# Loading the first segment's query and key weights in two pieces each from one queue

## The chip, the cores and the metric

The kernel runs on one core of a Trainium2 chip. The metric is the device time of one execution in microseconds. Six executions of the kernel before were timed; their median is 254.56 us, the lowest 253.71 and the highest 255.07.

## What is computed

A transformer block with conditioned normalization, on one sequence of 2048 rows of width 448, all in bfloat16:

```python
mod = silu(c) @ w_mod                       # six vectors of 448: sa, ca, ga, sb, cb, gb
h = layernorm(x) * (1 + ca) + sa
x = x + ga * A(h, wq, wk, wv, wo, beta)     # attention
h = layernorm(x) * (1 + cb) + sb
x = x + gb * B(h, w_gate, w_up, w_down)     # (sigmoid(h @ w_gate) * (h @ w_up)) @ w_down
```

The attention A has 16 heads of width 28 and works on 4 segments of 512 rows. Within a segment it is causal softmax attention; besides, each segment reads a memory (a 28 by 28 matrix and a vector for each head) that the segments before have written, and the two results are mixed by sigmoid(beta). The weights wq, wk, wv and wo are 448 by 448 each. w_gate and w_up are 448 by 1792, w_down is 1792 by 448.

## The kernel before

The engines' instruction streams are laid out by hand. Each engine works its stream off in order; semaphores that the framework inserts hold an instruction until its operands are there. A transfer (DMA) is issued by SP or by ScalarE from its own stream, so an issue stands behind whatever is ahead of it there. The framework signals the completion of transfers on eight semaphores that take turns: a transfer is issued only when the one that had its semaphore before, eight transfers earlier in the order that the framework settled, has landed.

A width of 448 is handled as four chunks of the contraction: three of 128 rows and one of 64 (`LW`). The work is staged by segment. For each segment x is normalized and transposed to hT, then q, k and v are projected (`proj_qk`, line 338, `proj_v`, line 350), then for each group of four heads the logits, their exponential, the mask and the product with v follow; the second half of the block follows a segment later, filled in between the attention steps from a list of jobs whose costs and due times are constants in the code (`tick`, `later`, `run_fill`). None of these constants depends on a transfer.

The change lies in the start, in the first 17 us. Lines 106 to 124 issue the first loads: the conditioning vector c_col on ScalarE, two tiles of x on SP and two on ScalarE, and the modulation weights wm for ca and sa in halves, one half on each queue. ScalarE then computes a tanh of c_col (line 126). Lines 151 to 156 load wq, wk and wv: wq and wk into staging tiles `wq_st` and `wk_st`, which lie in the memory that w_down is loaded into later (so the profile names them `wd_sb`), wv into its place. In the kernel before, wq and wk come in three pieces each, chunks 0 and 1, chunk 2, and chunk 3. All of wk's are issued by SP, of wq's the first by SP and the other two by ScalarE.

While these come in, PE runs 20 matmuls without use for their result (`warm_up`, line 645), VectorE normalizes the first four tiles of x (lines 672 to 684), PE computes the modulation columns (`mod_cols`, line 215) and transposes the normalized tiles (`ln0_tr`, line 687). Then the weights are prepared:

```python
    for k in range(2):
        pad_copy(nc.vector, wq_sb, wq_st, k)
    ln0_tr(2)
    ln0_tr(3)
    for kc in range(NK):
        ln0.pe_evac(pts[kc], kc, True)
        if kc == 1:
            pad_copy(nc.vector, wq_sb, wq_st, 2)
    evac_q, evac_k = bias_rows((wq_st, wk_st))
    pad_copy(nc.vector, wq_sb, wq_st, 3)
    warm_up(1)
```

`pad_copy` (line 650, profiled at line 657) scales one chunk of a weight by the modulation and spreads it into heads of 32 columns. `bias_rows` (line 659, profiled at line 664) multiplies the shift vector sa with all four chunks of wq and wk on PE, chunk by chunk, so it reads wq chunk k and wk chunk k side by side. The two rows that result are copied into the 65th row of chunk 3 of `wq_sb` (`evac_q`, on ScalarE) and of `wk_sb` (`evac_k`, on VectorE; both profiled at line 668). wk's four `pad_copy` stand between the two. The first projections (lines 712 and 713) follow, then the same for wv (lines 714 to 719), then the loads of x for segments 1 and 2 (lines 720 and 721). All later loads are issued by SP: beta and wm for ga (line 732), wo (line 160), the last segment of x, w_down (line 746), and w_gate and w_up (lines 741 and 742).

Of the kernel before, what the change touches and what calls it, by code (L numbers as in the profile page):

```python
# [13 lines left out]
P = 128  # L14
# [3 lines left out]
def kernel(  # L18
# [16 lines left out]
    nc = tc.nc  # L35
    _, S, D = A_x.shape
# [7 lines left out]
    DP, LW = NK * P, D - 3 * P  # L44
# [92 lines left out]
    wq_st = wd_sb[:, 0:NK, :]  # L137
    wk_st = wd_sb[:, NK:2 * NK, :]

    def load_w(eng, dst, w):  # L140
        eng.dma_start(dst[:, 0:3, :], w[0:3 * P, :].rearrange("(k p) n -> p k n", p=P))
        eng.dma_start(dst[0:LW, 3, :], w[3 * P:D, :])
# [6 lines left out]
    for b in wm_bufs:  # L149
        nc.vector.memset(b[:, NK * D:], 0.0)  # L150
    for st, w in ((wq_st, A_wq), (wk_st, A_wk)):
        other = nc.scalar if w is A_wq else nc.sync
        nc.sync.dma_start(st[:, 0:2, :], w[0:2 * P, :].rearrange("(k p) n -> p k n", p=P))
        other.dma_start(st[:, 2, :], w[2 * P:3 * P, :])
        other.dma_start(st[0:LW, 3, :], w[3 * P:D, :])
    load_w(nc.sync, wv_sb, A_wv)

    def load_wo():
# [557 lines left out]
    for k in range(NK):  # L716
        r = P if k < 3 else LW
        w = wv_sb[0:r, k, :]
# [156 lines left out]
```

## Time and profile before

| What | Value |
|---|---|
| median of six timed executions | 254.56 us (253.71 to 255.07) |
| the profiled execution, its own time | 254.45 us |
| its span, first to last instruction | 252.7 us |
| mean granted clock of TensorE | 0.993 |
| busy: PE, VectorE, ScalarE, GpSimd | 242.2, 173.8, 139.0, 73.8 us |
| moved by transfers | 19.66 MB, of which 17.61 MB on q1 (SP's queue) and 1.72 MB on q10 (ScalarE's) |
| moved in the first 40 us | 10.26 MB, 257 GB/s on average |

A profile is one execution, and its times run from the start of the span. In a timeline a line holds the start, the duration, the engine, the line of the code, the operation, and output and input; SPq and ACTq are the issues of transfers by SP and ScalarE, PEld are PE's weight loads, and DVE is VectorE. What stands in brackets is the idle time before, and who ended it. A transfer's issue is short; when its data has landed is read from the semaphore events of the trace. The DMA queues are called q1 and q10 there.

### The profile page before, as it was taken

To read this page: it belongs to the slowest core of one execution; us is meant where nothing else is said; L and a number is where in the kernel's file an instruction comes from. 1 tells how busy PE (TensorE), PEld (TensorE's weight loads), DVE (VectorE), ACT (ScalarE), POOL (GpSimd) and SP (SyncE) were. 2 spreads that over 40 slices of the span, in tenths; PEclk is the share of its full clock that TensorE was granted. 3 is DMA by queue.
4 is the path that set the end of the run, shared out by engine and by line. 5 is a ranking of instruction groups with operands and counts; after the bars stand their busy time and mean duration, and the time that the engine had idled before them with its cause. 6 is when DMAs were issued, how large, how long until landed. Compare 5 with 4: busy or idle time off the path is not lost.

```text
span 252.7 us, 5315 instructions
## 1 busy us (share of the span) xinstructions
PE 242.2 (96%) x2059; PEld 115.1 (46%) x2083; DVE 173.8 (69%) x419; ACT 139.0 (55%) x173; POOL 73.8 (29%) x140
## 2 busy tenths in 40 slices
PE   7999999999987999999999999999999999999995
PEld 2534545446533345445434355454344455333454
DVE  6878799874987686389868666895565486544412
ACT  2158879988894978575466857552653300133300
POOL 4359144233552221335613141471120023000000
PEclk9999999999997999999999999999999999999999
DMA  5999996495034212102532210113210015100011
GB/s 151 290 261 250 354 275 112 87 184 72 3 64 66 48 38 21 23 0 44 99 79 44 42 23 0 23 31 92 57 22 3 0 23 119 36 0 0 3 36 36
DMA packets 41168, 19.66 MB, mean 78 GB/s; under 512 B 30008, under 2 KB 40248, under 8 KB 41144
## 3 DMA queue, kind: packets, MB, share of 16 engines
q1 hardware_dynamic: 38408, 17.61, 31.6%
q10 hardware_dynamic: 2736, 1.72, 2.4%
q8 instruction: 16, 0.26, 0.4%
q14 instruction: 8, 0.07, 0.1%
HBM read 10.67 MB, written 1.84 MB: 49 GB/s over the span
## 4 chain that ended last, share of the span: by engine, by line
PE 51%; DVE 7%; POOL 1%; issue 1%; DMA 1%; ACT 1%; DVEq 0%; POOLq 0%
PE ups L559 13%; PE dps L574 13%; PE gps L542 12%; PE gps L547 5%; PE acc L451 3%; PE pwo L510 2%; PE lg L424 2%; DVE fT L562 1%; DVE st L269 1%; DMA hT<-xn 1%; DVE x_sb L520 1%; DVE t L482 1%; PE dM L397 1%; PE ups L547 1%; PE mem L475 1%
## 5 line engine op out<-in xcount | busy, mean ns | idle before, releaser
L427 ACT ACTIVATE pT<-lg 128x2048 bf16<-128x2048 f32 (+1 forms) x48 | 76.8, 1601 | 25.8 <-PE lg L424 25.5
L562 DVE SCALAR_TENSOR_TENSOR fT<-tt,ups 128x512 bf16<-128x512 f32 x56 | 37.3, 687 | 40.4 <-PE ups L559 38.5
L550 ACT ACTIVATE tt<-gps 128x512 f32<-128x512 f32 x56 | 30.4, 594 | 56.4 <-PE gps L547 56.4
L437 POOL TENSOR_SCALAR_AFFINE_SELECT pT<-pT 128x512 bf16<-128x512 bf16 x64 | 40.6, 651 | 70.1 <-ACT pT L427 70.1
L574 PE MATMUL dps<-wd_sb,fT 128*128 128x448 bf16 (+1 forms) x238 | 43.7, 342 | 0.0
L542 PE MATMUL gps<-hT,wg_sb 128*128 128x512 bf16 x155 | 41.0, 387 | 1.6 <-DVE hT L291 0.6
L559 PE MATMUL ups<-hT,wu_sb 128*128 128x512 bf16 x165 | 40.6, 381 | 0.4 <-issue 0.3
L574 PEld LDWEIGHTS <-fT 128*128 128x128 bf16 x238 | 22.9, 98 | 18.7
L542 PEld LDWEIGHTS <-wg_sb 128*128 128x128 bf16 x168 | 15.9, 99 | 18.6 <-issue 1.3
L559 PEld LDWEIGHTS <-wu_sb 128*128 128x128 bf16 x168 | 14.1, 97 | 21.7 <-issue 7.9
L451 PE MATMUL acc<-vt,pT 128*128 128x29 bf16 x640 | 18.6, 175 | 2.0 <-POOL pT L437 1.7
L269 DVE BATCH_NORM_STATS2 st<-x_sb 128x6 f32<-128x448 bf16 x32 | 19.7, 616 | 0.5
L451 PEld LDWEIGHTS <-pT 128*128 128x128 bf16 x640 | 17.7, 96 | 5.1 <-POOL pT L437 2.4
L547 PE MATMUL ups<-hT,wgu_sb 64*128 64x512 bf16 x56 | 18.1, 389 | 0.8 <-ACT tt L550 0.5
L273 POOL TENSOR_SCALAR rs<-mv 128x1 f32<-128x1 f32 (+2 forms) x21 | 5.3, 251 | 44.8 <-DVE mv L270 43.7
L424 PE MATMUL lg<-qT,kT 28*128 28x512 bf16 (+3 forms) x256 | 17.3, 302 | 0.3 <-ACT pT L427 0.2
L547 PE MATMUL gps<-hT,wgu_sb 64*128 64x512 bf16 x56 | 17.2, 388 | 0.1
L343 PE MATMUL pq<-hT,wq_sb 128*128 128x512 bf16 x59 | 16.3, 379 | 0.5 <-issue 0.3
L343 PE MATMUL pq<-hT,wk_sb 128*128 128x512 bf16 x62 | 16.3, 379 | 0.1
L576 DVE TENSOR_TENSOR ot<-dps,x_sb 128x448 bf16<-128x448 f32 (+1 forms) x17 | 9.9, 591 | 9.0 <-PE dps L574 9.0
L277 DVE TENSOR_SCALAR xn<-x_sb,mv,rs 128x448 bf16<-128x448 bf16 x32 | 14.4, 471 | 2.3 <-POOL rs L274 2.3
L274 POOL TENSOR_TENSOR rs<-rs,mhalf 128x1 f32<-128x1 f32 (+2 forms) x21 | 14.2, 674 | 1.8
(101 smaller groups left out, 258.0 us busy)
## 6 DMA issues: line engine op xcount, KB each, us to landing
wm<-in_w_mod_dram SPq DMA_DIRECT2D x4, 392.0 KB, 5.7
x_sb<-in_A_x_dram SPq DMA_DIRECT2D x3, 448.0 KB, 5.7
wd_sb<-in_B_w_down_dram SPq DMA_DIRECT2D x3, 448.0 KB, 9.5
wg_sb<-in_B_w_gate_dram SPq DMA_DIRECT2D x3, 448.0 KB, 9.8
wu_sb<-in_B_w_up_dram SPq DMA_DIRECT2D x3, 448.0 KB, 10.2
out_dram<-ot SPq DMA_DIRECT2D x8, 112.0 KB, 1.8
out_dram<-ot ACTq DMA_DIRECT2D x7, 112.0 KB, 1.7
wm<-in_w_mod_dram SPq DMA_DIRECT2D x2, 196.0 KB
```

What stands on the lines that cost most here:

```text
L269: nc.vector.bn_stats(st[:], self.srcs[i])
L343: nc.tensor.matmul(pq[:, 0:L], lhsT=head_cols(w_sb, k, hc), rhs=h[:, k, :], start=(k == 0), stop=(k == NK - 1))
L424: nc.tensor.matmul(lg[:, hs, wid:wid + nq], lhsT=kT[r, hc, kb * P:(kb + 1) * P], rhs=qT[r, hc, kb * P:L], start=True, stop=True, tile_posi ...
L427: nc.scalar.activation(pT[:, :, w0:w0 + wid], lg[:, :, 0:wid], AF.Exp, scale=scale)
L437: nc.gpsimd.affine_select(out=blk, in_=blk, compare_op=ALU.is_ge, fill=0.0, base=0, pattern=[[0, 4], [1, P]], channel_multiplier=-1)
L451: nc.tensor.matmul(accv[:, qb, hs, 0:ME], lhsT=pT[:, hs, c0:c0 + P], rhs=vt[:, kb, hc * 4 + hs, 0:ME], start=(kb == 0), stop=(kb == qb))
L542: nc.tensor.matmul(g[:, 0:L], lhsT=wg_sb[:, k, f], rhs=h[:, k, :], start=(k == 0), stop=False)
L547: nc.tensor.matmul(dst[:, 0:L], lhsT=wgu_sb[r:r + LW, f], rhs=h[r:r + LW, 3, :], start=first, stop=not first, tile_position=(r, 0))
L550: nc.scalar.activation(tt[:], g[:, 0:L], AF.Tanh, scale=0.5)
L559: nc.tensor.matmul(u[:, 0:L], lhsT=wu_sb[:, k, f], rhs=h[:, k, :], start=False, stop=(k == 2))
L562: nc.vector.scalar_tensor_tensor(ft[:], tt[:], 1.0, u[:, 0:L], op0=ALU.add, op1=ALU.mult)
L574: nc.tensor.matmul(dp[:, c], lhsT=fT_of[(s, fc)][:, t * P:(t + 1) * P], rhs=wd_sb[:, fc, c], start=(fc == 0), stop=(fc == NFC - 1))
```

## The change

wq and wk come in two pieces each instead of three: one of chunks 0 to 2 and one of chunk 3 with its 64 rows. The order is wq's large piece, wk's large piece, wq's small piece, wk's small piece, and SP issues all four. ScalarE issues no transfer any more after the modulation weights until the outputs of the last segments. The destinations and everything that reads them are as before.

```diff
     for st, w in ((wq_st, A_wq), (wk_st, A_wk)):
-        other = nc.scalar if w is A_wq else nc.sync
-        nc.sync.dma_start(st[:, 0:2, :], w[0:2 * P, :].rearrange("(k p) n -> p k n", p=P))
-        other.dma_start(st[:, 2, :], w[2 * P:3 * P, :])
-        other.dma_start(st[0:LW, 3, :], w[3 * P:D, :])
+        nc.sync.dma_start(st[:, 0:3, :], w[0:3 * P, :].rearrange("(k p) n -> p k n", p=P))
+    for st, w in ((wq_st, A_wq), (wk_st, A_wk)):
+        nc.sync.dma_start(st[0:LW, 3, :], w[3 * P:D, :])
     load_w(nc.sync, wv_sb, A_wv)
```

## The prediction

> **What bounds the kernel now.** I read the page first: engine shares and slices.
>
> ```profile
> PE   7999999999987999999999999999999999999995
> PEclk9999999999997999999999999999999999999999
> ...
> DMA  5999996495034212102532210113210015100011
> ```
>
> Each digit is a fortieth of the span. By the page's first part TensorE (PE) is busy for 242.2 us, 96% of the span; after the first slice it has one weak spot, slices 12 and 13 (76 to 88 us), where its granted clock falls too. The DMA engines are full from about 2 us on, in the stage this change touches. An edit to the loads is therefore worth what it does to the start of PE's work, unless it empties or fills a hole later. So I went next to the waits of PE: over the whole run no transfer is named in them; the longest is that weak spot (us in total, times, longest).
>
> ```profile
> PE acc L451 <- POOL pT L437: 1.7, 1, 1.7
> ```
>
> A wait of under 0.2 us doesn't get a line there, so I read the timeline of the first 17 us, the DMA issues first.
>
> ```profile
> 2.38 0.47 SPq L153 DMA_DIRECT2D wd_sb<-in_A_wq_dram  x1
> 4.63 0.38 SPq L153 DMA_DIRECT2D wd_sb<-in_A_wk_dram  x1
> 5.06 0.47 SPq L154 DMA_DIRECT2D wd_sb<-in_A_wk_dram  x1
> 6.08 0.56 SPq L155 DMA_DIRECT2D wd_sb<-in_A_wk_dram  x1
> ...
> 6.36 0.35 ACTq L154 DMA_DIRECT2D wd_sb<-in_A_wq_dram  x1
> 8.12 0.52 ACTq L155 DMA_DIRECT2D wd_sb<-in_A_wq_dram  x1
> ```
>
> wq's last rows are issued last, from ScalarE's queue at 8.12, after all of wk. The trace names the semaphore of each issue: eight take turns, so each transfer waits until the eighth before it has landed. The 8.12 issue waited for half of the first modulation load (landed 8.10, by the semaphore events), the 6.36 issue for another (6.34). In the same way wk's first piece waited for c_col (4.62). wq's last rows land at 12.42. Their readers on VectorE (DVE) and PE:
>
> ```profile
> 11.38 0.42 DVE L306 COPY hT<-lntr 128x512 bf16<-128x512 bf16 x1
> 11.72 0.33 DVE L657 TENSOR_SCALAR wq_sb<-wd_sb,cols 128x448 bf16<-128x448 bf16 x1
> 11.97 0.42 DVE L306 COPY hT<-lntr 128x512 bf16<-128x512 bf16 x1
> 12.45 0.33 DVE L657 TENSOR_SCALAR wq_sb<-wd_sb,cols 64x448 bf16<-64x448 bf16 x1
> ...
> 12.32 0.22 PEld L664 LDWEIGHTS <-sa_bf 64*1 64x1 bf16 x2 [0.38 <-issue]
> ...
> 12.47 0.35 PE L664 MATMUL warm<-wd_sb,sa_bf 64*1 64x448 bf16 x2
> ...
> 15.59 0.08 PEld L664 LDWEIGHTS <-sa_bf 64*1 64x1 bf16 x1 [0.38 <-issue]
> ```
>
> Both start 24 and 42 ns after the landing. Without a wait they would start sooner: the first hT copy is followed after 0.34 us (11.38 to 11.72), the second only after 0.48 (11.97 to 12.45), so DVE stood 0.14 us. On PE, wv's rows have the same step with its data long there (landed 12.84): its last matmul starts 2 ns after its weight load at 15.59, wq's 147 ns after its own at 12.32. So PE stood 0.145 us. That is the only place where I find a consumer waiting for these loads.
>
> [...]the two ScalarE issues cost 0.35 + 0.52 us there. [...]from 6.3 to 6.5 us q1 (SP) moved 49 packets and q10 (ScalarE) 22. [...]The trace shows one such stretch of 3.41 us at half clock, after a stretch with 1.92 us of PE work.
>
> **The change part by part.** Durations are of the profiled execution: 254.45 us, of which 252.7 are span and 1.75 lie around it; it is 0.11 below the median of 254.56.
>
> *ScalarE's two issues go.* 0.87 us leaves its queue at 6.36 to 8.65. Its next work is the hT copy at 11.44, which waits for PE's transposes (6.6 us idle). Worth nothing.
>
> *SP's issues.* Four for wq and wk before (0.47, 0.38, 0.47, 0.56), four after. SP pays nothing more.
>
> *When the pieces land.* I count 896-byte rows in order of issue. Up to the modulation loads 1408 rows are ahead, in both kernels. Before: wq's first piece ends at row 1664 (landed 9.06), wk's at 1920 (9.80), 2048 (10.26), 2112 (10.69), wq's third 128 rows at 2240 (10.88), wv at 2624 (12.11), wq's tail at 2688 (12.42), wv's tail at 2752 (12.84). After: wq's 384 rows end at 1792, wk's at 2176, the tails at 2240 and 2304, wv at 2688 and 2752. Reading these from the same curve (estimates): wq 9.06 + 128 rows at 347 rows per us = 9.43; wk about 10.8; a 64-row tail took 0.3 to 0.44 us behind its forerunner, so wq's tail 11.2 and wk's 11.6 at the late end; wv 12.8 and 13.2. Their issues don't hold them up: wk waits for c_col as before (4.63), the tails for the first two x loads (5.06, 6.08), wv for modulation loads (6.64, 7.46).
>
> *Who needs them.* wq's first rows: DVE at 10.71, 1.3 us later. They land 0.37 later than before, hidden by the normalization and modulation work that DVE does until 10.86. wk: the bias rows on PE at 11.66, 0.9 us after; it lands 1.0 us later than wk's first piece did, and that 0.9 is all the cover. Beyond it each late us costs one. wq's tail: 12.31, margin 1.1. wk's tail: 12.32, margin 0.7. wv: 14.79, margin 1.6.
>
> *The wait that goes.* 0.145 us on PE and 0.14 on DVE, side by side, so counted once. What follows hangs on it step by step: warm matmul 12.75, evacuation of the q row on ScalarE 13.18, last q weights 13.75, k row on DVE 13.79, last k weights 14.47, kT copy 15.04, wv rows 14.93, next projection 15.87. Each is released by the one before, or follows in its queue without a gap; none of them waits for a transfer. So all move up 0.145. What is late next is PE's own step between weight loads of different height (0.28 us) and DVE's copies: no further gain.
>
> *Two transfers fewer, so the turns of the eight semaphores shift.* x for segments 1 and 2 are issued at about 8.10 and 8.80 instead of 9.33 and 9.97, beta at 9.43 instead of 10.52; the next modulation load still waits for PE's transposes (11.15), and from there each transfer has the same forerunner as before. Segment 1's x lands at 14.04 before and by 14.4 after; DVE wants it at 15.50. Does SP stall on a full queue? It issued at once with 2432 rows outstanding (17.40) and took 2.57 us with 2832 (17.83). At 8.80 the new kernel has 3776 issued less 1408 landed, 2368: no. If it did, beta, modulation and wo loads would slip, the first of them wanted at 22.1 us (beta, on ScalarE; landed 15.97). DMA total traffic is the same, and the gate and up weights land at 39 us, wanted from 79. Nothing.
>
> Sum: -0.145 us; 254.45 becomes 254.3, and the median 254.56 becomes 254.4. The bounds of the one unknown cost, DMA timing: in an execution where PE's clock rises earlier than at 7.37 us, the chain could reach wq's tail sooner, at most 0.25 more before DVE and GpSimd's normalization binds (norm at 10.03 to 10.42 against the sa copy at 10.70); where it rises later, the 0.145 vanishes. So -0.4 to 0, and I take the profiled value.
>
> **Rivals.** *A, forecast:* 254.4, own range 254.0 to 254.8.
>
> *B, the wait changes owner:* wk's tail, now behind wq's, lands as late as wq's did (12.4), and the bias row waits for it instead: 254.56. For: tails of 64 rows are slow for their size. Against: it would need 0.8 us more than estimated.
>
> *C, faster through the clock:* PE's half-clock stretch disappears.
>
> ```profile
> 72.22:75.64 3.42, 2.61 (x21) 1.10 (x18) 2.82 (x9) 3.42 (x5) 2.62 (x5) 1.00 0.30 61
> 75.64:79.05 3.41, 1.92 (x44) 1.32 (x44) 2.07 (x6) 2.98 (x4) 2.06 (x4) 1.00 0.42 87
> 79.05:82.46 3.41, 3.18 (x9) 0.87 (x10) 3.15 (x11) 0.08 (x1) 0.00 (x0) 0.50 0.41 38
> ```
>
> The stretches, with PE busy first after their length and the clock third from the end: 1.92 of 3.41 us busy (56%) was followed by half clock, 2.61 (76%) was not. A program 0.145 us earlier puts less of the hole at 74.83 to 76.50 into the window: 60%. If the limit lies between, 3.18 us of PE work runs at full clock: -1.6, giving 252.8. [...]
>
> *D, slower, through one mechanism:* the time to land grows with the size of a piece. wq's first piece took 6.7 us for 224 KB; at 336 KB in proportion 10.0, landing at 12.4 where DVE wants it at 10.71. Both q pads slip by 1.7, less the 0.145: 254.56 + 1.5 = 256.1. It decides from a landing after 10.71. Against: wv's 336 KB piece took 4.6 us (7.48 to 12.11); the 6.7 was queueing.
>
> That the change isn't what it says can hardly be: each piece is an instruction of its own.
>
> **How the numbers follow.** 0.3% of 254.56 is 0.76 us, about what a measurement of this kernel can tell from no change. A 0.46 and B 0.12 lie within it: same 0.58. C 0.25: faster. D 0.17: slower. The range reaches from C's time down to A's and B's: 252.7 to 255.4, leaving out D.
>
> **What would show it.** Right: no ScalarE issue of wq; the pad of wq's tail 0.34 us after the hT copy and the bias matmul right at its weight load; the first logits at 16.7 instead of 16.84. Wrong: DVE's first pad after 10.8, or a bias row at 11.66 that waits for wk (D); a gap before the last bias matmuls (B); full clock at 79 us (C).

## The result and the profile after

The changed kernel takes 253.64 us in the median of 34 timed executions (252.95 to 254.33). The kernel before, run beside it, has a median of 254.18 us (71 executions), and beside the experiments 254.09 to 254.23 in four sets of 19 to 51, all 0.3 to 0.5 below the median of the six that were shown first. The ratio of after to before is 0.9977, 95% interval 0.9967 to 0.9986: 0.58 us less, between 0.36 and 0.84. A later set of the changed kernel gave 0.9978 (0.9963 to 0.9993). The forecast was 254.4, 0.145 us below the time before: its sign is right, its size is a quarter of what came.

The profiled execution of after takes 253.97 us, with a span of 252.3 and a mean granted clock of 0.991. The page's slices of after:

```profile
PE   7899999999988999999999999999999999999995
PEclk9999999999997999999999999999999999999999
...
DMA  5999996493036330102331210113210015100011
```

The picture is the old one: one weak spot in slices 12 and 13, where the clock falls. The longest wait of PE that the kernel itself can do something about is still the mask at that spot, now line 450.

```profile
PE acc L450 <- POOL pT L436: 1.7, 1, 1.7
```

The issues of wq and wk in the timeline of after (start, duration, queue):

```profile
2.38 0.47 SPq L152 DMA_DIRECT2D wd_sb<-in_A_wq_dram  x1
4.65 0.38 SPq L152 DMA_DIRECT2D wd_sb<-in_A_wk_dram  x1
5.08 0.56 SPq L154 DMA_DIRECT2D wd_sb<-in_A_wq_dram  x1
5.98 0.47 SPq L154 DMA_DIRECT2D wd_sb<-in_A_wk_dram  x1
```

By the semaphore events they land at 9.30, 10.70, 10.96 and 11.35, wv at 12.20 and 12.51. The readers of wq's last rows, on VectorE (DVE) and on PE:

```profile
11.74 0.41 DVE L305 COPY hT<-lntr 128x512 bf16<-128x512 bf16 x1
12.07 0.32 DVE L656 TENSOR_SCALAR wq_sb<-wd_sb,cols 64x448 bf16<-64x448 bf16 x1
```

```profile
1.42 6.51 PE L646 MATMUL warm<-qT,ident 128*128 128x512 bf16 x20 [1.42 <-POOL mhalf L168]
...
11.43 1.01 PE L663 MATMUL warm<-wd_sb,sa_bf 128*1 128x448 bf16 x8
...
16.46 0.40 PE L423 MATMUL lg<-qT,kT 28*128 28x512 bf16 x4
```

The pad now follows the copy after 0.33 us, as every other pad does, where it was 0.48: the wait is gone. All eight bias matmuls run as one group without a hole. The first logits stand at 16.46, against 16.84 before, which is 0.38 and not 0.145. The other 0.23 comes from the clock: the 20 matmuls at the start took 6.51 us here and 7.41 in the profile before, because PE's clock rose at 5.55 instead of 7.37, and so the last hT copy starts at 11.74 instead of 11.97. That is not the change's doing; the rise differs from execution to execution, from 4.38 us (seventh experiment) to 7.37 in the profiles. It does show how little one profile says of this wait: the chain that reads wq's tail was ready 0.23 us sooner here.

At the weak spot the stretches of after are these (PE busy first after the length, clock third from the end):

```profile
70.41:73.82 3.41, 3.41 (x24) 1.60 (x22) 2.76 (x9) 3.41 (x5) 1.16 (x3) 1.00 0.27 55
73.82:77.23 3.41, 1.74 (x51) 1.25 (x50) 2.75 (x7) 3.41 (x6) 2.29 (x4) 1.00 0.39 79
77.23:80.64 3.41, 3.22 (x11) 1.22 (x9) 3.06 (x8) 1.02 (x2) 1.27 (x2) 0.50 0.92 83
```

So the half-clock stretch is still there in this execution. It begins 71.68 us after the clock's rise, as it did before (7.37 to 79.05, 5.55 to 77.23): 21 times 3.413 us, which is the length of the half-clock stretch itself in the clock records of both traces. But not every execution has it. The mean clock of each listed execution tells: 0.998 to 1.0 without the stretch, 0.993 or less with it (in the profiles 0.993 in before and 0.991 in after, with it, and 1.000 in the third and the seventh experiment, without). Of 166 executions of before, 55 (33%) are without; of 71 of the changed kernel, its repetition and one near relative (the seventh experiment), 35 (49%). Without it after takes 253.05 (median of 17), with it 254.04 (median of 18).

One further line of the two timelines matters, as the experiments came to show. It is the first multiplication of the next normalization by DVE, whose rows come by four transposing transfers (before, then after):

```profile
78.35 1.62 DVE L291 TENSOR_SCALAR hT<-hT,cols 128x512 bf16<-128x512 bf16 x4 [1.21 <-DMA hT<-xn]
```

```profile
77.43 1.90 DVE L290 TENSOR_SCALAR hT<-hT,cols 128x512 bf16<-128x512 bf16 x4 [0.66 <-DMA hT<-xn]
```

It is 0.92 us earlier, with the stage only 0.37 us earlier. The last of the four transposes landed at 77.78 before and at 77.40 after: DVE began 0.57 us after the landing before, and 0.03 us after it now.

### The profile page after: what moved, and what is told of

Its sections match the earlier page's. It is cut to its first block, busy times and chain, and to the rows that moved or that the text cites. A ratio compares the mean times of both kernels' runs of the same rounds, so it can differ in the third digit from the quotient of the medians.

```text
span 252.3 us, 5313 instructions
## 1 busy us (share of the span) xinstructions
PE 241.3 (96%) x2059; PEld 115.2 (46%) x2083; DVE 174.3 (69%) x419; ACT 139.1 (55%) x173; POOL 73.7 (29%) x140
## 4 chain that ended last, share of the span: by engine, by line
PE 50%; DVE 9%; issue 1%; POOL 1%; DMA 1%; ACT 1%; DVEq 0%; POOLq 0%
PE ups L558 13%; PE dps L573 13%; PE gps L541 11%; PE gps L546 5%; PE acc L450 2%; PE pwo L509 2%; PE lg L423 2%; DVE fT L561 2%; DVE st L268 1%; DMA hT<-xn 1%; DVE x_sb L519 1%; DVE t L481 1%; PE dM L396 1%; PE ups L546 1%; PE mem L474 1%
## 5 line engine op out<-in xcount | busy, mean ns | idle before, releaser
L276 DVE TENSOR_SCALAR xn<-x_sb,mv,rs 128x448 bf16<-128x448 bf16 x32 | 14.4, 471 | 2.6 <-POOL rs L273 2.6
```

## The experiments

The expectations number the theories. Theory 1: the lateness of wq's last rows costs what the change gains, more than 0.145 us in executions whose clock rises early. Theory 2: the half-clock stretch at the weak spot is what differs. Theory 3: it is the number of pieces, or ScalarE's issuing as such. Theory 4 came later: with two transfers fewer, the later loads lag less.

**First, the tail earlier in the kernel before.** ScalarE's two wq issues go ahead of its tanh.

```diff
-    nc.scalar.activation(th[:], c_col[:], AF.Tanh, scale=0.5)
 ...
     load_w(nc.sync, wv_sb, A_wv)
+    nc.scalar.activation(th[:], c_col[:], AF.Tanh, scale=0.5)
```

> The kernel before with one move: ScalarE's tanh stands behind its two wq issues, so that these no longer wait for it. Pieces and queues stay as before. Theory 1 (the last rows of wq land too late, by an amount that varies from one execution to the next, and this alone is the gain): the tail should land near 11 us instead of 12.4, and the time be that of the changed kernel, some 0.2% below before (253.6 against 254.2). Theory 2 (the gain comes from the half-clock stretch at 79 us being absent more often, by the shifted start): also a gain, since the start shifts alike; the two are not told apart here. Theory 3 (the number of pieces or ScalarE's issuing as such costs): no gain, 254.2.

Measured: 255.46 us (254.36 to 256.90), ratio 1.0052 (1.0028 to 1.0076). It was badly designed. The tanh's table load moved with it, behind issues that themselves wait for forerunners (timelines of ScalarE and DVE):

```profile
6.21 0.54 ACTq L154 DMA_DIRECT2D wd_sb<-in_A_wq_dram  x1
6.77 1.28 ACT L155 ACT_TABLE_LOAD   x1 [6.77 <-DMA x_sb<-in_A_x_dram]
8.07 0.20 ACT L155 ACTIVATE th<-c_col 112x4 f32<-112x4 bf16 x1
```

```profile
8.30 0.17 DVE L200 TENSOR_SCALAR th<-th 112x4 f32<-112x4 f32 x1 [1.52 <-ACT th L155]
```

DVE stood 1.52 us for the tanh. The run says nothing about wq's tail.

**Second, the tail late again in the changed kernel.** SP issues wq's last rows behind wv's large piece.

```diff
-    for st, w in ((wq_st, A_wq), (wk_st, A_wk)):
-        nc.sync.dma_start(st[0:LW, 3, :], w[3 * P:D, :])
-    load_w(nc.sync, wv_sb, A_wv)
+    nc.sync.dma_start(wk_st[0:LW, 3, :], A_wk[3 * P:D, :])
+    nc.sync.dma_start(wv_sb[:, 0:3, :], A_wv[0:3 * P, :].rearrange("(k p) n -> p k n", p=P))
+    nc.sync.dma_start(wq_st[0:LW, 3, :], A_wq[3 * P:D, :])
+    nc.sync.dma_start(wv_sb[0:LW, 3, :], A_wv[3 * P:D, :])
```

> The changed kernel with wq's last 64 rows issued by SP behind wv's large piece, so that they are again the 2688th row in order; two pieces each, and ScalarE issues none. Theory 1 (lateness): the gain is gone, 254.2, with the pad of wq's tail again right after the landing at about 12.4. Theory 3 (number of pieces or issuing queue): the gain stays, 253.6. Theory 2 (clock): back to before as well, since the start shifts back.

Measured: 254.14 us (253.53 to 254.91, 14 executions), ratio 1.0002 (0.9985 to 1.0018). The gain is gone, and the wait is back, in PE's timeline and in DVE's:

```profile
12.34 0.35 PE L664 MATMUL warm<-wd_sb,sa_bf 64*1 64x448 bf16 x2 [0.18 <-DMA wd_sb<-in_A_wq_dram]
```

```profile
12.32 0.33 DVE L657 TENSOR_SCALAR wq_sb<-wd_sb,cols 64x448 bf16<-64x448 bf16 x1 [0.17 <-DMA wd_sb<-in_A_wq_dram]
```

Against the runs of the changed kernel and its repetition the mean is 0.52 us higher (0.24 to 0.79). So with this one small transfer late again the gain is lost, though the count of transfers is the changed kernel's.

**Third and fourth, the hole at the weak spot filled,** in before and in the changed kernel, by six matmuls whose result is overwritten and of no use. That was the aim; as the line below shows, they run right behind the hole and not in it.

```diff
+        if u == (1, 1):
+            for _ in range(6):
+                nc.tensor.matmul(acc[:], lhsT=ident[:], rhs=kT_of[s][:, hc, :], start=True, stop=True)
```

> The kernel before with six matmuls of no use to the result (1.3 us of PE) put into the 1.7 us hole of PE at 74.8 us, so that the half-clock stretch behind it should not come. Theory 1 (lateness at the start): this kernel is faster than before by about half of the 1.0 us that lies between the two groups of times of the changed kernel, 253.6, and stays 0.2% above the same filling of the changed kernel. Theory 2 (clock share): it falls to the changed kernel's better group, 253.0, and the two filled kernels are equal.

> The changed kernel with the same six matmuls in the hole at 74.8 us. Theory 1: 253.0 in all executions, the better of its two groups, and 0.5 us below the filled kernel before. Theory 2: 253.0, equal to the filled kernel before. If the filling delays the product that follows it, both filled kernels lose alike.

Measured: before with the fill 253.60 (253.28 to 254.51), ratio 0.9985 (0.9974 to 0.9997); changed with it 253.61 (253.45 to 255.62), ratio 0.9996 (0.9975 to 1.0018). Full clock in 21 of 22 and in 14 of 14 executions, against 33% and 49% without the fill: six wide matmuls more behind the hole take the half-clock stretch away. The fill itself costs about half a microsecond (253.6 against 253.05 in the changed kernel at full clock), since the matmuls wait for their buffer, and the products with v start at 77.37 instead of 76.13 (line from the timeline of the fourth):

```profile
76.06 1.47 PE L447 MATMUL acc<-kT,ident 128*128 128x512 bf16 x5 [1.61 <-DVE t L484]
```

By their medians the two filled kernels are equal, as theory 2 said and theory 1 did not, though at 253.6 and not at the 253.0 of theory 2. Four of the 14 executions of the fourth are at 255.3 to 255.6 at full clock, which I can't explain. The third's profile happens to have an early rise of the clock (5.32), and shows what the tail's wait is then (PE's list of waits):

```profile
PE warm L667 <- DMA wd_sb<-in_A_wq_dram: 0.5, 1, 0.5
```

From there on its ScalarE is 0.57 us behind that of the changed kernel, whose clock rose at 5.55. So the wait that I took at 0.145 is 0.57 in such an execution.

**Fifth and sixth, 26 warm-up matmuls instead of 20,** so that the chain arrives later than wq's tail in either kernel.

```diff
-    NWARM, EARLY, KEEP = 20, 2400.0, (0, 2, 1, 3)
+    NWARM, EARLY, KEEP = 26, 2400.0, (0, 2, 1, 3)
```

> The kernel before with 26 warm matmuls at the start instead of 20, which keeps PE from beginning its real work until about 9.1 to 10.0 us (8.1 to 8.7 with 20). Theory 1 (the landing of wq's last rows at 12.4 is a floor under the start, and it costs the more the earlier PE is ready): the pad of the tail comes at 12.7 or later, waits for nothing (0.34 us after the hT copy), and this kernel takes as long as the changed kernel with 26, about 255. Theory 3 (pieces or queue as such): it stays 0.2% above it.

> The changed kernel with 26 warm matmuls. Theory 1: about 255, within 0.1 of the kernel before with 26; the change is worth nothing when PE is late. Theory 3: 0.5 below it.

Measured: 254.61 (253.72 to 256.62), ratio 1.0026 (1.0004 to 1.0048), and 254.50 (253.06 to 256.61), ratio 1.0009 (0.9984 to 1.0033). Neither profile has the wait. The two times scatter over 3 us, so they can't tell 0.1 from 0.3 us between the kernels. Inconclusive.

**Seventh, the tail back on ScalarE's queue in the changed kernel.**

```diff
-        nc.sync.dma_start(st[0:LW, 3, :], w[3 * P:D, :])
+        (nc.scalar if w is A_wq else nc.sync).dma_start(st[0:LW, 3, :], w[3 * P:D, :])
```

> The changed kernel with one of the four issues, wq's last 64 rows, back on ScalarE behind its tanh. Theory 1: what counts is when the tail lands. If its turn of the semaphores lets it be issued by 6.4, it lands before 11.8 and the time is that of the changed kernel, 253.6; if it lands at 12.4 it is that of before. Theory 3 (ScalarE's issuing as such costs): 254.2 whenever it lands.

Measured: 253.69 us (253.03 to 255.41), ratio 0.9984 (0.9966 to 1.0003). wq's tail lands at 11.01, nobody waits, and the time is near that of after. That ScalarE issues costs nothing that these 14 executions show, as predicted. ScalarE issued the tail at 4.83 here, against 8.12 in before, where its forerunner on the semaphore landed at 8.10: what made it late there was its turn, and not ScalarE's queue as such.

**Eighth and eleventh, three pieces as before, all on SP.** One set of executions each.

```diff
-        other = nc.scalar if w is A_wq else nc.sync
+        other = nc.sync
```

> The kernel before with all six pieces issued by SP, wq's three and then wk's three. Theory 1: wq's tail lands near 10 us, all of wk before 11.8, and the time is that of the changed kernel, 253.6 (0.2% below before), with three pieces each. Theory 3: the number of pieces costs, so at most half of the gain.

> The kernel with three pieces each, all issued by SP, once more. Theory 1: 253.6; the 254.1 seen the first time was chance, from which executions the half-clock stretch and the collisions of VectorE with GpSimd fell into. Theory 4: 254.1 again.

Measured: 254.29 (253.20 to 255.34), ratio 1.0002 (0.9986 to 1.0019), and 254.07 (253.12 to 255.40), ratio 1.0001 (0.9980 to 1.0021). Yet wq's tail lands at 9.95 in the eighth, and DVE pads it without a wait, right behind the copy:

```profile
11.73 0.42 DVE L306 COPY hT<-lntr 128x512 bf16<-128x512 bf16 x1
12.06 0.32 DVE L657 TENSOR_SCALAR wq_sb<-wd_sb,cols 64x448 bf16<-64x448 bf16 x1
```

That was the blow to theory 1: the wait is gone, the start equals that of after, and there is no gain. What these kernels share with before is the count of transfers.

**Ninth and tenth, the changed kernel with wv in four pieces, and the changed kernel once more.** The ninth keeps the change and has as many transfers as before.

```diff
-    load_w(nc.sync, wv_sb, A_wv)
+    for k in range(3):
+        nc.sync.dma_start(wv_sb[:, k, :], A_wv[k * P:(k + 1) * P, :])
+    nc.sync.dma_start(wv_sb[0:LW, 3, :], A_wv[3 * P:D, :])
```

> The changed kernel with wv in four pieces instead of two, so that there are as many transfers as before and x for segments 1 and 2 is issued as late as before; wq's and wk's loads stand ahead and aren't touched. Theory 1 (only the landing of wq's tail counts): the time of the changed kernel, 253.6. Theory 4 (formed on seeing the kernel with three pieces each from SP keep the time of before, though in its profile nothing waited for the tail: the two transfers fewer, which let all later ones be issued sooner, are the gain or half of it): 254.1.

> The changed kernel once more, beside the others of this group on one chip. All theories: 253.6, 0.2% below before; the share of executions with a half-clock stretch near one half.

Measured: 253.90 (252.90 to 256.34), ratio 0.9988 (0.9968 to 1.0008), and 253.61 (253.00 to 254.70), ratio 0.9978 (0.9963 to 0.9993). By the means, the two extra transfers cost the changed kernel 0.45 us (0.06 to 0.86). The ninth's profile seemed to say where (PE's list of waits):

```profile
PE pq L344 <- DMA hT<-xn: 0.8, 1, 0.8
```

In it the last up weights land at 41.21, the transposes for segment 2 queue behind them, and PE stands 0.8 us. The eighth's transposes had landed only 0.1 us before PE wanted them (42.32 and 42.42), those of after 0.74 before. Theory 4 looked good.

**Twelfth, its test: three pieces all on SP, with the last two up weights issued at 57 us.**

```diff
-[piece(wu_sb, B_w_up, k) for k in range(NK)]
+[piece(wu_sb, B_w_up, k) for k in range(2)]
...
-    fill.extend(j2[8:] + j3[:2] + m[0][1:] + [(2000, prep_b2)] + j3[2:])
+    fill.extend(j2[8:] + sp(piece(wu_sb, B_w_up, 2)) + sp(piece(wu_sb, B_w_up, 3)) + j3[:2] + m[0][1:] + [(2000, prep_b2)] + j3[2:])
```

> The kernel with three pieces for wq and wk each, all on SP, but with the last two pieces of the up weights (128 and 64 rows of 1792) issued by SP at about 57 us, where the DMA engines have room, instead of at 28.7 and 29.4 us. In the kernel with three pieces these last pieces landed at 40.24 in one execution and 39.59 in another; the transposes of segment 2's rows, behind them in the same queue, landed their fourth at 42.32 and 41.69, and PE wanted it at 42.42: a margin of 0.1 us in one of the two, against 0.74 in the changed kernel. In the kernel with wv in four pieces they landed at 41.21 and PE waited 0.78 us. Theory 4 (the lag of later loads, in part of the executions, is what takes the gain from the kernel with three pieces): the fourth transpose lands by 41.7 whatever the loads do, the executions of 254.7 us and more become rare (7 of 28 before), and the ratio to the kernel before is about 0.998, as the changed kernel's 0.9977. Rival (the number of pieces costs in another place, or by chance): ratio 1.000, 254.2 us, with a quarter of the executions at 254.7 and more. If the moved loads delay the attention's own transposes near 58 us, it shows as a PE wait there.

Measured: 254.27 us (252.95 to 255.16, 14 executions), ratio 1.0001 (0.9981 to 1.0021). The transposes landed at 41.67, 0.74 before PE wanted them, and still nothing was gained. Theory 4 falls as the cause of the lost gain, as far as 14 executions tell. It remains a way in which single executions lose 0.8 us.

But the twelfth's trace shows where the kernels part. Its ScalarE runs within 0.01 us of that of after up to 77 us. Because two issues are moved from about 29 us to 57 us, its turns of the semaphores are those of after in between, and those of before only from 57 us on. Then DVE and PE (two timelines of the twelfth):

```profile
77.96 1.64 DVE L291 TENSOR_SCALAR hT<-hT,cols 128x512 bf16<-128x512 bf16 x4 [1.19 <-DMA hT<-xn]
```

```profile
77.14 0.92 PE L355 MATMUL pv<-wv_sb,hT 128*128 128x448 bf16 x4
78.69 1.46 PE L542 MATMUL gps<-hT,wg_sb 128*128 128x512 bf16 x3 [0.64 <-DVE hT L291]
```

The same lines of the seventh kernel, with the changed kernel's count of transfers:

```profile
77.50 1.84 DVE L290 TENSOR_SCALAR hT<-hT,cols 128x512 bf16<-128x512 bf16 x4 [0.71 <-DMA hT<-xn]
```

```profile
77.16 0.92 PE L354 MATMUL pv<-wv_sb,hT 128*128 128x448 bf16 x4
78.11 0.39 PE L541 MATMUL gps<-hT,wg_sb 128*128 128x512 bf16 x1
78.75 1.35 PE L541 MATMUL gps<-hT,wg_sb 128*128 128x512 bf16 x5 [0.25 <-DVE hT L290]
```

The four transposes landed at 77.41 in the one and at 77.48 in the other, but DVE began at 77.96 and at 77.50. The waiting instructions on DVE's queue, which the page doesn't count as work, stand in the trace with their semaphores. In brackets is when the transposes on these landed:

```
before    77.81 waits S103 (77.78)   78.24 waits S108, S102 (71.63, 75.82)   78.35 multiplies, waits S100 (73.16)
after     76.38 waits S107 (72.80)   76.82 waits S108, S106 (75.43, 71.25)   77.43 multiplies, waits S100 (77.40)
twelfth   77.43 waits S103 (77.41)   77.86 waits S108, S102 (71.26, 75.46)   77.96 multiplies, waits S100 (72.79)
```

The same wait of before for the last segment:

```
before   215.33 waits S104 (215.31)  215.40 waits S108, S102 (211.18, 214.66) 215.50 multiplies, waits S100 (212.74)
```

DVE waits for four semaphores in three instructions, in an order fixed by the framework. At 78 us it takes 0.43 us from the first to the second, and 0.11 more to the multiplication, even where all has long landed. The eight semaphores (S100 and S102 to S108 in the traces) take turns over the transfers. With two fewer at the start, the four transposes sit two places earlier in the turn. The last to land is now on S100, which the multiplication itself waits for, and the 0.54 us pass before the landing. Before, it was on S103, the first waited for, and they come after it. From the landing of the last transpose to DVE's start, by kernel:

| transfers as many as before | us | two fewer | us |
|---|---|---|---|
| before | 0.57 | changed | 0.03 |
| first (tail early) | 0.55 | | |
| third (fill) | 0.57 | second (tail late) | 0.03 |
| fifth (26 warm-ups) | 0.57 | fourth (fill) | 0.03 |
| eighth, eleventh (three pieces) | 0.55, 0.57 | sixth (26 warm-ups) | 0.03 |
| ninth (wv in four) | 0.55 | seventh (tail on ScalarE) | 0.03 |
| twelfth | 0.55 | tenth (changed again) | 0.03 |

The 0.43 us is not the price of such a waiting instruction in general: at 215 us the same step takes 0.07 us. Why it is long at 78 us in all three kernels (0.43 or 0.44 us) stays open. The renumbering moves the start at 215 us too (0.20 us behind the landing in before, 0.03 in after), but PE doesn't stand there.

What PE loses by it is seen at full clock in an equal stretch of the seventh kernel and of the eighth (PE busy first):

```profile
75.00:78.41 3.41, 2.22 (x45) 1.44 (x46) 2.54 (x7) 3.02 (x4) 2.27 (x4) 1.00 0.32 67
```

```profile
75.00:78.41 3.41, 1.92 (x44) 1.33 (x44) 2.07 (x6) 3.02 (x4) 2.27 (x4) 1.00 0.38 77
```

0.3 us less work in the stretch: the hole at the weak spot is wider. Directly that costs 0.27 us (ScalarE at 80.45 and 80.72), and by 132 us these two executions have given it back. What it costs depends on where the half-clock stretch falls. With the stretch from 77.2 or 77.3 on, the eleventh loses 0.11 us against after between 77 and 82 us; before and the twelfth, whose stretch begins at 79.05 and 78.54, lose 0.62. No profile of a kernel with two fewer has so late a stretch to set beside these. With the fill behind the hole nothing is lost there (third against fourth, 0.01 us).

So the traces show the later start of DVE and the wider hole. That these are what takes the gain from the kernels with the old turns is the best account of the times, but it is argued from the groups of executions, and not shown step by step.

## Why the prediction was right, and where its size came from

**The wait that goes.** The mechanism was right at the start: the wait on wq's tail is gone on PE and DVE, and the first logits come earlier. The term of the sum was mis-sized. The 0.145 belongs to one execution in which the clock rose at 7.37; the third kernel shows 0.57 where it rose at 5.32. The prediction saw this ("where PE's clock rises earlier than at 7.37 us, the chain could reach wq's tail sooner, at most 0.25 more") and took the profiled value all the same; its bound was 0.17 short too.

**The step that failed is "Two transfers fewer, so the turns of the eight semaphores shift",** with its end "DMA total traffic is the same ... Nothing". It followed the turns into each transfer's forerunner and into SP's queue, which was right: x was issued at 7.96 and 8.76 (forecast 8.10 and 8.80) and landed at 13.86 (by 14.4). It did not follow them to the readers, whose order of waiting is tied to the semaphores and not to the landings. The 64 executions without the tail's wait but with the old turns (eighth, ninth, eleventh, twelfth) have a mean of 254.11; the 71 with neither have 253.63: 0.47 less (0.26 to 0.70).

**The two together.** By the means, before is at 254.13. The tail early but the old turns (eighth, eleventh, twelfth): 254.14, 0.0 from before, with 0.2 either way. The new turns but the tail late (second): 254.12. Both: 253.60. Neither alone gains what can be measured; together they gain half a microsecond. So the one step that the prediction counted, by itself, is worth 0.0 with 0.2 either way: this leaves room for the forecast 0.145, and not for what was measured. That the sign came out right, and the time inside the stated range, is in part luck. 253.64 lies outside the 254.0 to 254.8 of the forecast itself; the whole range holds it because it reached down to C. A part of the distance is that the six executions shown first have a median 0.38 above that of the 71 beside the result.

The split by clock says how the 0.50 between before and the 71 is made up. Executions without the stretch are 253.54 on average before and 253.16 in the 71, those with it 254.43 and 254.10; 0.35 of the 0.50 lies within these two groups. The share without a stretch has risen by 16 points, and that is worth 0.15. With the second kernel's 14 executions I can't say whether the sizes add up exactly. A kernel in which only the order of DVE's waits is changed was not tried; it would be the direct test.

**The rest.** ScalarE's issues: worth nothing (seventh). Landings: wq 9.30 (forecast 9.43), wk 10.70 (10.8), wq's tail 10.96 (11.2), wk's 11.35 (11.6), wv 12.20 and 12.51 (12.8 and 13.2). The row count erred on the late side only, and B (wk's tail takes over the wait) and D (the larger piece lands after 10.71) had nothing to stand on. C came half true. The stretch goes in more executions than before, and in those the kernel is near C's 252.8 (253.05). But C's reason, 0.145 us against a limit in busy time, is not shown to be it: the clock rises at 7.37, 5.55 and 4.38 us in before, after and the seventh, while PE's first matmul stands at 1.42 in all three, and the half-clock stretch of the first two begins 71.68 us after the rise. Up to 3 us from one execution to the next leave nothing to see of a shift of 0.145. What the traces show changed is the hole.

## What to carry to other kernels

Count the transfers, not only their bytes: where completions take turns on a few semaphores, an edit to the number of transfers at the start renumbers every later one, and a reader that waits for several at once may then have the last to land first in its order of waits, here 0.55 us at 78 us for an edit at 5 us, because the step between the waiting instructions is long at this place (0.43 us); at 215 us, where it is 0.07 us, it was 0.17 us. Look for it as a start well after the last landing, not as a long wait. And before a sum rests on one short wait, ask what in that execution set the arrival of the waiting side; here the phase of the clock moved it between 0.145 and 0.57 us.

## What the runs showed of the hardware

The busy time that the profile counts doesn't by itself decide the half clock. In the seventh kernel a stretch with 1.82 us of PE work (16 large matmuls, from 72.64, which is 20 times 3.413 us after its clock's rise at 4.38) was followed by full clock, and so was one with 1.81 us in the third (16, from 73.59). In before one with 1.92 us was followed by half clock; 40 of its 44 matmuls were the products with v, with 29 columns each.

Nor was PE idle in a stretch that half clock followed: of 3.41 us it was busy for 1.92 in before, 1.74 in after and 1.72 in the tenth.

A DVE multiplication beside GpSimd's mask took 0.71 us instead of 0.29, in two profiles at the same place (after, then before). Which it is hangs on who begins first. In after the mask had begun at 132.66; in before DVE was first, and the mask, begun at 133.65, took 0.74 us instead of 0.63. In all 14 profiles it goes by this: 0.66 to 0.71 us in ten where the mask was first, 0.29 in four where DVE was. In after it cost 0.42 us of a lead that on ScalarE fell from 0.98 us at 133 us to 0.45 at 140:

```profile
132.73 0.71 DVE L368 TENSOR_SCALAR r<-qT 128x512 bf16<-128x512 bf16 x1
```

```profile
133.60 0.29 DVE L369 TENSOR_SCALAR r<-qT 128x512 bf16<-128x512 bf16 x1
```
